# A transformer block on one core: the last 256 queries as two units of 128, with one second feed-forward product for both

## The chip, the core and the metric

The kernel runs on one core of a Trainium2 chip. The time is device microseconds (us) of one execution of the program. Beside the times of three runs there is one profiled execution, whose trace gives the start and the end of the instructions on each engine: PE (TensorE matmuls, with weight loads listed as PEld), ACT (ScalarE), DVE (VectorE), POOL (GpSimd) and SP (SyncE, which here issues every DMA).

## What is computed

A pre-norm transformer block over 2048 tokens of width 1024, in bf16:

```python
h  = x + attention(layernorm(x), wqkv, wo)     # 32 heads of 32 columns, full softmax, no mask
h2 = h + gelu(layernorm(h) @ w1 + b1) @ w2 + b2  # inner width 3584, gelu in its tanh form
```

The layer norm has no learned scale. Scores are multiplied by 32 to the power −1/2 before the softmax.

## The kernel before

**Tasks, a planner and fixed orders.** The code does not emit instructions straight away. Each call of `pe`, `mm`, `act`, `dve`, `pool` and `dma` adds a task to a graph, with the buffers that it reads and writes, an estimated duration (`c_act` for ACT, literal numbers for others), a priority and a kind (`qk`, `exp`, `pv`, `den`, `bg` for background, `warm`). `schedule` plays the graph through with these estimates and so fixes one order for each engine; `pick_pe` decides which ready task PE takes next. Two strings of digits (`PV_BEGIN`, `PV_MUST`) tell it, for each group, how many finished rounds of exponentials may pile up before P·V must run, and two tables (`GROUP_SHIFT`, `PRIO_SHIFT`) shift single tasks in the order. `merge_tiles` turns runs of narrow matmuls (four of 32 columns side by side) that are long enough into whole ones of 128. `assign` then sets the semaphores. On the chip every engine follows its fixed order and waits where a semaphore says so.

**Units, groups and rounds.** The queries are cut into `UNITS`, 8 units of 256. The heads form 8 groups of 4. For each unit and group there is a `Job` of 8 rounds. A round (`Att.qk`, L955) does 8 score matmuls, each with 32 rows of K and Q (four heads side by side in the array), into four PSUM banks, and two exponentials of 128x1024 on ACT (L966) into a buffer PT. Three pairs of score banks are used in turn. Later follow 8 narrow matmuls P·V (L1010), the sums of P over keys on DVE (L1027; for the first six units a second addition, L1033, joins two rounds) and narrow matmuls with ones for the denominators (L1050). `finish` (L1058) divides and writes OT. There are 512 rounds in all.

**What runs beside attention.** For each unit u, after its attention: `wo(u)` (product with Wo, four blocks of 512 KB, plus the residual), `ln2(u)`, `ffn1(u)` (14 blocks W1 of 256 columns; DVE adds b1 at L1206; `gelu` is made of DVE operations and a Tanh on ACT, L1229) and `ffn2(u, j, ...)` for two column halves j (14 blocks W2; DVE adds the residual at L1258, then the output DMA). These background matmuls (L660 narrow, L663 whole) fill PE between the scores of later units. They come one unit or more behind: FFN2 of unit 6 is still running when the last exponentials end.

**The lead.** Tiles x of 128 tokens are loaded by `x_tile`, normalised by `layer_norm` (DVE, with a power on POOL at L732), transposed on PE (`tr_tile`, `transposes`, L759) and copied from PSUM to xnT on ACT (L766) or DVE. `proj_half` makes Q and K of the first group in halves, `proj` and `proj_v` all other projections. `N_WARM` matmuls on constants (L1275) keep PE busy before the first tile is there.

**The tail.** The last unit, b = unit 7, is finished when no attention is left to hide it. Its W1 blocks lie in a second ring R2, whose 14 buffers are laid over the space of K and V of the groups: block i needs group i//2 to be done in b's attention. `wo(b, True)` does the first six groups (`WSPLIT`) early, and the last two, with an identity matmul that adds the residual, after the last group. `ln2(b, True)` takes its statistics from PSUM and transposes on PE (L745). `ffn1(b, ws1, True)` does its first three blocks (`HALVES`) in token halves of 128 and the others on 256; their gelu is one ACT operation straight from PSUM (L1212). `ffn2(b, ...)` puts its four results into banks 0 to 3. The whole matmuls of the tail are at L666. Unit 6 (a) goes through the ordinary path: its FFN1 loads its own 14 W1 blocks and runs during b's exponentials.

All DMAs are issued on SP in one order; a DMA that must wait for its source or its buffer holds back those behind it.

Of the kernel before, what the change touches and what calls it, by code (L numbers as in the profile page):

```python
# [7 lines left out]
ACT = mybir.ActivationFunctionType  # L8
# [59 lines left out]
class Graph:  # L68
# [267 lines left out]
    def emit(self, e, obj):  # L336
# [10 lines left out]
PV_BEGIN = "7577886548677765858856674434636846646566545566645345783555878553"  # L347
PV_MUST = "4534436267554436543436636337557333354424733246352322524333334446"
GROUP_SHIFT = (
        "0:116 1:277 2:281 4:-80 5:7 6:-257 7:-169 10:-74 14:-10 16:11 19:28 23:-117 25:-15 26:-52 27:-7 "  # L350
        "28:-94 34:-63 36:-9 44:46 46:112 47:57 52:-28 53:53 54:62 55:-11 56:1 57:-184 58:-28 60:-22 63:-28 "
        "64:16 65:-118 68:-25 70:8 76:161 79:-82 80:102 81:5 82:-25 85:27 86:-404 87:111 88:-41 90:-21 92:29 "
        "93:-269 99:-184 100:-38 103:-107 109:1 114:-32 115:20 118:-67 119:-26 120:27 121:20 122:-20 "
        "125:-349 128:2 133:-6 134:-4 135:-5 136:-96 138:-3 139:13 144:-23 145:-64 154:5 155:17 156:132 "
        "157:199 159:-154 161:12 167:-6 170:-17 171:-149 173:104 174:-24 175:117 179:-64 180:-24 188:21 "
        "189:-8 191:-351 199:-12 202:-228 205:21 206:-63 207:176 208:179 209:-139 219:28 220:-127 221:-46 "
        "223:-15 225:96 226:-29 227:-294 230:4 234:1 235:18 236:55 237:44 238:87 248:29 249:-176 253:-9 "
        "254:19 256:-139 257:-3 258:-224 260:-158 261:5 262:16 264:43 266:-2 267:14 268:9 269:157 278:-40 "
        "279:-33 280:-29 281:-23 282:-15 287:6 289:-106 290:16 291:11 293:42 294:9 297:-29 298:116 299:-16 "
        "308:-7 309:-67 310:15 311:179 312:-207 313:86 315:54 317:-242 319:-442 321:150 325:108 327:256 "  # L360
        "328:330 329:19 330:-25 331:214 332:94 336:136 337:-51 ")
PRIO_SHIFT = (
        "0:-1 2:1 4:-1 8:1 10:-1 53:1 54:1 55:-1 57:-2 58:-1 59:1 60:-3 61:-1 63:1 66:1 88:1 127:1 135:1 "
        "137:1 138:1 140:1 150:1 190:2 194:-1 196:-2 198:-1 200:-2 226:2 228:-1 258:-1 260:-2 261:-1 264:-1 "
        "267:-2 268:-2 269:-1 270:-2 271:-1 292:1 332:-1 381:1 386:-1 388:-1 389:1 390:1 392:-1 418:-1 "
        "442:-1 447:1 448:1 450:-1 472:-2 478:-1 499:-1 500:2 506:3 507:1 508:1 509:-1 527:-1 528:2 603:-3 "
        "654:1 671:1 688:1 725:-1 726:1 746:2 749:-1 770:-1 780:-1 784:1 786:-1 788:1 796:2 803:1 806:-3 "
        "810:4 815:-2 822:-1 830:-2 839:-1 840:1 841:1 842:-1 869:2 929:-1 995:-2 1062:1 1104:1 1109:1 "
        "1133:1 1144:-1 1156:-1 1161:3 1162:1 1168:-1 1174:-2 1180:-1 1198:1 1199:2 1200:1 1206:1 1208:-1 "
        "1210:-1 1213:-2 1214:1 1220:2 1222:-2 1225:3 1226:-1 1228:-1 1234:-3 1238:-1 1244:2 1249:1 1252:1 "  # L370
        "1262:-1 1265:-1 1266:-1 1268:-1 1274:1 1277:1 1278:-1 1289:-1 1290:1 1296:1 1301:2 1302:1 1303:-1 "
        "1322:2 1383:-1 1400:-1 1417:2 1422:-1 1449:-2 1458:1 1465:-1 1466:-1 1468:-3 1469:2 1472:2 1474:-1 "
        "1477:1 1483:1 1486:1 1489:-1 1494:-1 1495:1 1510:2 1517:-1 1519:1 1520:-2 1539:1 1548:-1 1557:1 "
        "1566:-1 1600:1 1636:-2 1650:-1 1654:-1 1666:-1 1671:1 1674:-1 1682:-1 1684:-1 1686:4 1688:-1 "
        "1694:-1 1702:-1 1706:1 1712:2 1723:2 1724:-1 1726:-1 1730:1 1737:1 1756:-1 1765:-1 1817:-1 1834:1 "
        "1851:-1 1859:1 1862:1 1864:1 1868:3 1876:-2 1877:-1 1880:1 1888:1 1889:1 1903:-3 1906:1 1908:-1 "
        "1917:-1 1920:2 1926:2 1932:1 1935:1 1941:-2 1951:-2 1952:-1 1953:-1 1955:-2 1973:-1 1982:-2 2000:-1 "
        "2034:-1 2051:-2 2068:-1 2076:2 2088:2 2090:-1 2093:1 2100:1 2112:1 2129:-1 2147:1 2199:-1 2233:1 "
        "2247:-1 2250:1 2281:-1 2282:1 2284:1 2285:1 2294:-1 2303:-1 2321:1 2330:2 2332:-1 2340:-3 2343:-1 "
        "2352:-1 2355:2 2356:1 2362:1 2367:-1 2368:1 2374:-2 2381:-1 2398:-1 2402:2 2404:-1 2410:-1 2420:-1 "  # L380
        "2434:1 2454:-1 2459:-1 2466:-1 2478:-1 2485:-1 2486:1 2488:-1 2499:-1 2506:-1 2520:-2 2523:1 2530:1 "
        "2534:-1 2536:1 2537:-2 2538:-2 2540:1 2582:-1 2593:-1 2594:3 2604:2 2608:-2 2628:1 2647:1 2648:2 "
        "2650:1 2651:-1 2656:-2 2659:-1 2660:1 2665:2 2670:-1 2711:-2 2743:-2 2744:-1 2754:1 2791:-1 2793:1 "
        "2794:1 2795:-1 2814:-1 2834:-2 2836:1 2837:-1 2856:-1 2874:-1 2876:2 2877:1 2878:1 2921:-1 2958:-1 "
        "2963:-1 3042:1 3043:-1 3045:-1 3046:1 3060:2 3072:1 3075:2 3084:1 3086:-1 3087:-1 3093:-1 3094:-1 "
        "3102:-2 3103:1 3116:-1 3128:2 3130:-1 3134:1 3142:-1 3146:1 3155:-1 3168:-1 3175:1 3181:1 3184:1 "
        "3187:1 3192:-1 3193:1 3209:-1 3211:1 3216:-1 3218:-1 3221:1 3222:-4 3228:-1 3233:-1 3246:-1 3248:-1 "
        "3256:1 3260:1 3261:1 3264:1 3272:1 3274:1 3281:1 3284:1 3293:1 3298:-2 3305:1 3306:-1 3315:-1 "
        "3322:1 3324:-1 3327:-2 3328:1 3330:-1 3334:-3 3340:2 3366:1 3380:-1 3390:1 3418:-1 3429:1 3430:2 "
        "3432:-1 3436:1 3496:1 3498:1 3500:-2 3533:-1 3563:1 3600:2 3604:1 3606:-2 3643:-1 3644:2 3648:-2 "  # L390
        "3688:-1 3690:-1 3730:1 3732:-2 3768:-1 3770:-2 3773:2 3792:-3 3814:-3 3816:-2 3856:1 3880:-2 "
        "3891:-2 3901:-2 3902:2 3912:1 3922:-1 3943:-1 3944:-1 3950:-2 3953:2 3958:-1 3968:1 3971:-1 3974:1 "
        "3986:1 3997:-1 4006:1 4008:-1 4012:2 4024:2 4026:-4 4038:-2 4042:-2 4050:-1 4064:-2 4065:1 4071:-1 "
        "4074:1 4083:-2 4095:-1 4098:-1 4104:-2 4105:-2 4114:-1 4117:-1 4124:1 4130:1 4132:-1 4141:-3 "
        "4142:-1 4148:1 4171:-1 4174:2 4177:1 4195:1 4201:-1 4204:-1 4211:-1 4212:-1 4213:2 4216:1 4226:-1 "
        "4235:1 4236:1 4242:-2 4244:-1 4258:1 4259:1 4262:2 4264:-1 4276:2 4306:2 4309:1 4310:-1 4312:-2 "
        "4313:-1 4314:1 4317:-1 4318:-1 4320:2 4330:-2 4332:-1 4394:1 4396:1 4398:1 4478:2 4496:2 4497:-1 "
        "4498:-2 4500:-1 4538:2 4542:-1 4580:-1 4583:1 4585:-1 4586:-1 4622:-2 4625:-1 4626:1 4665:-2 "
        "4750:-1 4763:1 4784:2 4799:-1 4807:1 4811:2 4824:-1 4828:1 4833:2 4836:-1 4845:1 4852:-3 4860:1 "
        "4861:1 4864:-2 4866:-1 4869:5 4874:-1 4875:1 4878:1 4881:1 4893:-1 4896:1 4899:2 4902:2 4908:-1 "  # L400
        "4916:1 4917:1 4922:-1 4927:1 4928:-1 4930:-1 4934:-1 4936:-1 4939:-1 4948:-7 4966:-1 4969:1 4981:-3 "
        "4984:1 4987:-1 4990:3 4999:-1 5005:-1 5012:1 5019:-1 5021:-1 5022:1 5030:-1 5034:1 5052:-1 5057:-2 "
        "5073:1 5075:2 5076:1 5078:-1 5081:2 5084:2 5086:2 5093:-1 5099:1 5102:1 5108:1 5110:2 5118:-1 "
        "5125:1 5128:-1 5148:-1 5151:-1 5158:1 5164:-1 5170:1 5174:1 5182:1 5201:-2 5202:-1 5220:-3 5222:1 "
        "5223:1 5224:-1 5225:2 5226:-1 5230:-1 5232:1 5235:-1 5236:-1 5237:-1 5239:1 5241:-1 5308:-1 5310:-1 "
        "5312:1 5314:-2 5316:2 5346:1 5375:1 5394:1 5413:1 5414:-1 5415:1 5416:-1 5459:-1 5478:-1 5499:1 "
        "5500:-1 5542:1 5604:-2 5646:1 5668:1 5674:1 5684:1 5691:1 5694:1 5700:1 5709:1 5723:-1 5726:-1 "
        "5730:1 5737:1 5740:-1 5744:-1 5746:-1 5749:-1 5750:-2 5752:-1 5761:2 5762:1 5776:1 5778:-1 5779:-3 "
        "5782:-1 5785:-1 5788:1 5797:2 5812:1 5821:-1 5824:-1 5829:1 5830:-1 5831:1 5836:1 5844:-2 5862:2 "
        "5868:-1 5882:1 5884:-1 5891:1 5897:1 5908:-1 5921:1 5935:-3 5937:-1 5942:1 5944:-1 5949:-2 5950:3 "  # L410
        "5961:-1 5962:1 5968:-2 5974:-2 5976:-1 5989:-1 5991:1 5994:-1 5997:-2 6003:1 6009:-1 6014:1 6024:1 "
# [30 lines left out]
def build_kernel(nc, A_x, A_wqkv, A_wo, B_w1, B_b1, B_w2, B_b2, out):  # L442
# [6 lines left out]
    G = D // P  # L449
    DC = D // P  # L450
    FC = F // P
    SCALE = DH ** -0.5
    EPS_BF = 1.0013580322265625e-05

    UNITS = [(256 * i, 256) for i in range(8)]
    NU = len(UNITS)

    def utiles(u):
        t0, n = UNITS[u]
        return range(t0 // P, (t0 + n) // P)  # L460

# [1095 lines left out]
```

## Time and profile before

| | |
|---|---|
| median of three runs | 1073.02 us (1071.93 to 1075.29) |
| profiled execution | 1071.41 us |
| its span in the trace | 1069.6 us |
| mean granted clock of PE in it | 0.998 |
| first scores (L955) start | 13.80 us |
| last scores start | 1006.15 us |
| last exponential ends | 1008.85 us |
| moved by DMA | 177.5 MB, mean 166 GB/s |

The span is the time from the first to the last instruction in the trace; the execution took 1.8 us more. Busy time of an engine is the union of its instructions. A group line of the profile gives line, engine, operation, the output and the inputs by the program's names, the tile, the count, then busy time, mean ns of one, and the idle time before them with what ended most of it. A line of the chain of waits gives shares of the span, followed back from the last instruction.

### The profile page before, as it was taken

Reading aid. Unit: us, or ns where it says so; the run is one execution under the profiler, and the core shown is the slowest. Engines: PE = TensorE matmul, PEld = TensorE weight load, DVE = VectorE, ACT = ScalarE, POOL = GpSimd, SP = SyncE. Lnnn points to the kernel's source line nnn. Section 1 sums busy time; section 2 is a strip of 40 time slices with the busy share of each in tenths; the row PEclk is TensorE's granted clock in tenths of the full one; section 3 lists DMA queues with packets and bytes.
Section 4 is the critical chain, followed back from the end, with each engine's and each line's share of the span. In section 5 each row is a group of like instructions: output and inputs, shape, how many; then the busy total and the mean of one; then the engine's idle time right before and its main releaser. Section 6 shows DMA issues by size and latency. Waiting matters only on the chain.

```text
span 1069.6 us, 40833 instructions
## 1 busy us (share of the span) xinstructions
PE 1028.5 (96%) x18417; PEld 593.4 (55%) x18469; DVE 836.2 (78%) x1654; ACT 1012.3 (95%) x1118; POOL 19.1 (2%) x36
## 2 busy tenths in 40 slices
PE   7899999999999999999999999999999999999998
PEld 5566645554446545744465456446645754564483
DVE  8857877777799997999699979979984986796611
ACT  5999999999999999999999999999999999999850
POOL 2100000000000000000000000000000000000000
PEclk9999999999999999999999999999999999999999
DMA  7920011004567587646776686588567745998640
GB/s 188 240 98 2 5 60 42 2 2 135 174 193 228 158 207 233 192 139 187 218 235 177 194 233 178 148 230 251 147 178 235 215 136 178 299 288 250 211 131 21
DMA packets 279999, 177.51 MB, mean 166 GB/s; under 512 B 41616, under 2 KB 274576, under 8 KB 279440
## 3 DMA queue, kind: packets, MB, share of 16 engines
q1 hardware_dynamic: 279824, 174.89, 56.5%
q8 instruction: 145, 2.38, 0.9%
q14 instruction: 30, 0.25, 0.1%
HBM read 160.96 MB, written 10.22 MB: 160 GB/s over the span
## 4 chain that ended last, share of the span: by engine, by line
ACT 70%; PE 24%; DVE 3%; DMA 2%; issue 0%; POOL 0%; POOLq 0%; SPq 0%
ACT PT L966 66%; PE ps L663 6%; PE ps L666 6%; PE ps L660 5%; PE ps L955 3%; ACT tg L1229 3%; PE ps L1010 2%; PE ps L1050 1%; DMA a_w1r<-in_B_w_dram 1%; DVE PS L1027 1%; DVE st L711 1%; DMA hnT<-a_xb 1%; PE ps L1275 1%; DMA q_scratch<-a_ost 0%; DVE xnT L768 0%
## 5 line engine op out<-in xcount | busy, mean ns | idle before, releaser
L966 ACT ACTIVATE PT<-ps 128x1024 bf16<-128x1024 f32 x996 | 924.4, 1140 | 4.1 <-PE ps L955 3.9
L1027 DVE TENSOR_TENSOR PS<-PT 128x1024 bf16<-128x1024 bf16 x425 | 288.1, 685 | 95.4 <-ACT PT L966 63.4
L955 PE MATMUL ps<-QT,KT 32*128 32x256 bf16 x4096 | 204.0, 273 | 10.1 <-ACT PT L966 4.9
L1010 PE MATMUL ps<-PT,V 128*32 128x256 bf16 x3984 | 166.9, 273 | 1.9 <-ACT PT L966 0.8
L955 PEld LDWEIGHTS ps<-QT,KT 32*128 32x128 bf16 x4096 | 61.0, 92 | 166.9 <-ACT PT L966 144.1
L663 PE MATMUL ps<-hnT,a_w1r 128*128 128x256 bf16 x1030 | 126.8, 273 | 3.9 <-DVE gT L1206 1.4
L1010 PEld LDWEIGHTS ps<-PT,V 128*32 128x32 bf16 x3984 | 101.2, 97 | 37.4 <-issue 6.5
L663 PEld LDWEIGHTS ps<-hnT,a_w1r 128*128 128x128 bf16 x1030 | 94.1, 98 | 32.2 <-issue 18.4
L660 PE MATMUL ps<-a_w2r,gT 128*32 128x512 bf16 x1560 | 110.0, 381 | 1.4 <-DVE OD L1085 1.0
L1033 DVE TENSOR_TENSOR PS<-PS 128x1024 bf16<-128x1024 bf16 x135 | 92.6, 686 | 2.5
L663 PE MATMUL ps<-a_w2r,gT 128*128 128x512 bf16 x367 | 89.7, 380 | 4.4 <-issue 2.7
L1050 PE MATMUL ps<-PS,ones 128*32 128x256 bf16 x1160 | 81.1, 274 | 0.9 <-DVE PS L1033 0.4
L660 PE MATMUL ps<-hnT,a_w1r 128*32 128x256 bf16 x2152 | 77.6, 274 | 3.2 <-DVE gT L1206 0.9
L1206 DVE TENSOR_TENSOR gT<-ps,b1f 128x512 bf16<-128x512 f32 x98 | 66.8, 686 | 13.5 <-PE ps L660 9.5
L660 PEld LDWEIGHTS ps<-hnT,a_w1r 128*32 128x32 bf16 x2152 | 52.2, 96 | 19.7 <-issue 16.0
L663 PEld LDWEIGHTS ps<-a_w2r,gT 128*128 128x128 bf16 x394 | 34.0, 98 | 45.8 <-issue 11.8
L1229 ACT ACTIVATE tg<-tg 128x1024 bf16<-128x1024 bf16 x49 | 54.7, 1144 | 0.0
L660 PEld LDWEIGHTS ps<-a_w2r,gT 128*32 128x32 bf16 x1560 | 34.8, 96 | 30.7 <-issue 16.0
L660 PE MATMUL ps<-xnT,Wall 128*32 128x512 bf16 x596 | 41.9, 381 | 0.4 <-DVE KT L820 0.3
L663 PE MATMUL ps<-Wall,xnT 128*128 128x256 bf16 x321 | 41.0, 273 | 0.0
L1050 PEld LDWEIGHTS ps<-PS,ones 128*32 128x32 bf16 x1160 | 30.9, 96 | 16.6 <-issue 5.3
L1258 DVE SCALAR_TENSOR_TENSOR b_ost<-ps,hch 128x512 bf16<-128x512 f32 x4 | 2.8, 692 | 45.0 <-PE ps L666 45.0
(99 smaller groups left out, 1022.8 us busy)
## 6 DMA issues: line engine op xcount, KB each, us to landing
a_w2r<-in_B_w_dram SPq DMA_DIRECT2D x105, 512.0 KB, 5.0
a_w1r<-in_B_w_dram SPq DMA_DIRECT2D x98, 512.0 KB, 4.6
a_w1r<-in_A_wo_dram SPq DMA_DIRECT2D x32, 512.0 KB, 4.4
b_w1r<-in_B_w_dram SPq DMA_DIRECT2D x14, 512.0 KB, 5.2
a_w1r<-in_A_wqkv_dram SPq DMA_DIRECT2D x11, 512.0 KB, 4.6
Wall<-in_A_wqkv_dram SPq DMA_DIRECT2D x16, 256.0 KB, 5.2
hch<-in_A_x_dram SPq DMA_DIRECT2D x16, 256.0 KB, 4.1
xrb<-in_A_x_dram SPq DMA_DIRECT2D x15, 256.0 KB, 4.5
```

The lines of the kernel that those rows point to most:

```text
L660: fns.append(lambda p, j=j: p.matmul(psum[32 * j:32 * j + 32, bi(bank), c0:c1], lhsT[:, 32 * j:32 * j + 32], rhs, start=start, stop=stop, ...
L663: t.whole = lambda p: p.matmul(psum[:, bi(bank), c0:c1], lhsT, rhs, start=start, stop=stop, skip_group_check=True)
L666: t = pe(lambda p: p.matmul(psum[:, bi(bank), c0:c1], lhsT, rhs, start=start, stop=stop), occ, reads=reads, writes=[bb(bank)], mode="full" ...
L711: return dve(lambda v: v.bn_stats(st_l[:, i, 6 * c:6 * c + 6], src), 0.6, reads=[B_src], writes=[B_stl[i][c]], prio=prio)
L955: return p.matmul(psum[:, 2 * us[h // 2] + h % 2, n * i:n * i + n], KT[32 * h:32 * h + 32, g, k0:k0 + P], QT[32 * h:32 * h + 32, qs, 0:n], ...
L966: act(lambda a, u=u, k=k: a.activation(pt(s)[:, k, :, :], psum[:, 2 * u:2 * u + 2, :], ACT.Exp, bias=0.0, scale=SCALE), 1024, reads=[B_ps[ ...
L1010: fns.append(lambda p, i=i, h=h: p.matmul(psum[32 * h:32 * h + 32, bi(bank), 0:nq], V[:, g, nk * r + i, 32 * h:32 * h + 32], pt(s)[:, h // ...
L1027: dve(lambda v: v.tensor_tensor(PS[:, n, :, :], pairs[:, :, 0:256], pairs[:, :, 256:512], ALU.add), c_dve(1024, 2), reads=[B_PT[2 * s], B_ ...
L1033: dve(lambda v: v.tensor_tensor(PS[:, n, :, :], PS[:, n, :, :], PS[:, m, :, :], ALU.add), c_dve(1024, 2), reads=[B_PS[n], B_PS[m]], writes ...
L1050: fns.append(lambda p, h=h, rhs=rhs, i=i: p.matmul(psum[32 * h:32 * h + 32, bi(bank), nq:2 * nq], ones32[:, :], rhs, start=False, stop=las ...
L1206: drop(dve(lambda v: v.tensor_tensor(gT[:, fc:fc + 2, cs], psum[:, bi(bank), 0:2 * n].rearrange("p (f c) -> p f c", f=2), b1f[:, fc:fc + 2 ...
L1229: act(lambda a: a.activation(t, t, ACT.Tanh, bias=0.0, scale=math.sqrt(2.0 / math.pi)), c, reads=B_t, writes=B_t, prio=-1)
```

## The change

The last unit is cut into two of 128 queries, so there are 9 units, and the last two are a (unit 7) and b (unit 8), together the old unit 7. Their jobs have 4 rounds of 16 score matmuls of 128 columns each, with 4 key blocks per round in place of 2; the number of rounds and exponentials in all stays as it was. The 14 blocks in the ring R2 (`ws1`) are now asked for before `ffn1(a, ws1)`, which uses them, and `ffn1(b, ws1, True)` uses them again. Results of `ffn1(a)` go through the DVE eviction into gT; their gelu is 7 new ACT operations of 128x512 (`late_gelu`), ordered behind the last exponential. One call `ffn2([a, b], j, ...)` serves both, with the W2 blocks that b had. The old unit 6 is an ordinary unit now, whose FFN2 takes the place of `ffn2(a)` in the code. `HALVES` goes away.

In the lead, x tile 1 is loaded in two DMAs, the transposes of the first two tiles are copied to xnT in two ACT operations of 512 each, and the first `proj_half` waits for each half on its own. `proj` and `proj_v` get a dependency on the end of the lead. `LEAD_DMA = 16` leaves a new branch in `tr_tile` unused.

The summing of P is written in a general form (`ROUNDS`, `part`, `parts`) with the same sums as before. In the planner, the estimates for an ACT operation (base 0.0615 to 0.05 us), for the power on POOL, for a warming matmul and for a change of tiling are altered, and all four tables are other ones.

```diff
-    UNITS = [(256 * i, 256) for i in range(8)]
+    UNITS = [(256 * i, 256) for i in range(7)] + [(1792, 128), (1920, 128)]
...
-        return 0.0615 + (0.093 if ap_bias else 0.0) + n / 1200.0
+        return 0.05 + (0.093 if ap_bias else 0.0) + n / 1200.0
...
+    LEAD_DMA = 16
+    B_half = [[gr.buf() for _ in range(2)] for _ in range(2)]
+    HALF = 2
...
+        if tt < HALF:
+            h = DC // 2
+            for dc in range(DC):
+                pe(lambda p, dc=dc: p.transpose(psb[:, bank, dc * P:(dc + 1) * P], xb[:, tt, dc * P:(dc + 1) * P], ident[:]),
+                   0.056, reads=[B_xb[tt], B_ident], writes=[B_ps[bank]], prio=prio)
+            for k in range(2):
+                act(lambda a, k=k: a.activation(xnT[:, tc, h * k:h * k + h, t4 * P:(t4 + 1) * P],
+                                                psb[:, bank, h * k * P:h * (k + 1) * P].rearrange("p (dc t) -> p dc t", dc=h), ACT.Copy), 512,
+                    reads=[B_ps[bank]], writes=[B_half[tt][k]] + ([B_xnTt[tc][t4]] if k else []), prio=-1)
+            return
...
-               [B_W[wp(blk)][c // P]] + B_xnTt[tc], True)
+               [B_W[wp(blk)][c // P]] + B_xnTt[tc], True, after=lead_end if dc == 0 else ())
...
-                   [B_W[wp(blk)][0]] + B_xnTt[tc][2 * h + c // P:2 * h + (c + n) // P], n > P, cols=(c, c + n))
+                   [B_W[wp(blk)][0]] + ([B_half[c // P][2 * dc // DC]] if hc == 0 and HALF else B_xnTt[tc][2 * h + c // P:2 * h + (c + n) // P]),
+                   n > P, cols=(c, c + n))
...
-                transposes_2(R.xb[s][:, :], R.B_xb[s], (4, 5), hnT[:, :, t * P:(t + 1) * P], B_hnT[t], 1 if t else -4)
+                transposes_2(R.xb[s][:, :], R.B_xb[s], (4, 5), hnT[:, :, k * P:(k + 1) * P], B_hnT[k], -4)
...
+            for f in range(2):
+                for dc in range(DC):
+                    ffn1_end[u] = mm(bank, w[:, dc, f * P:(f + 1) * P], hnT[:, dc, cs], dc == 0, dc == DC - 1,
+                       [B_w] + (B_hnT[hs[0]][2 * dc // DC:2 * dc // DC + 1] if tail else B_h), not tail, (n * f, n * f + n),
+                       after=ffn2_last if f == 0 and dc == 0 and not tail else ())
...
+    def late_gelu(u):
+        cs, hs = gcols(u)
+        for fc in range(0, FC, 4):
+            g = gT[:, fc:fc + 4, cs]
+            B_g = [B_gT[fc // 2 + k][hs[0]] for k in range(2)]
+            act(lambda a, g=g: a.activation(g, g, ACT.Gelu_apprx_tanh, bias=0.0, scale=1.0), 512, reads=B_g, writes=B_g, prio=1,
+                after=[last_exp()])
...
-    x_tile(1, -6)
+    x_tile(1, -6, 2)
...
     for j in range(2):
-        ffn2(a - 1, j, w2_blocks(R1, j))
-    ffn1(a)
+        ffn2([a - 1], j, w2_blocks(R1, j))
     ws1 = [wblock(R2, B_w1[:, 256 * i:256 * i + 256], 2) for i in range(14)]
+    ffn1(a, ws1)
     wo(b, True)
     ln2(b, True)
-    for j in range(2):
-        ffn2(a, j, w2_blocks(R1, j))
     ws2 = [w2_blocks(R2, 0), w2_blocks(R1, 1)]
+    late_gelu(a)
     ffn1(b, ws1, True)
     for j in range(2):
-        ffn2(b, j, ws2[j], banks=(2 * j, 2 * j + 1), half=False, R=R2)
+        ffn2([a, b], j, ws2[j], banks=(2 * j, 2 * j + 1), half=False, R=R2)
```

## The prediction

> **What bounds the kernel now.** I read the engine totals first, then the chain of waits, the costliest groups, the windows by stage, the waits, and last the timelines of TensorE in mid-kernel and of the end. Engine totals and chain:
>
> ```profile
> PE 1028.5 (96%) x18417; PEld 593.4 (55%) x18469; DVE 836.2 (78%) x1654; ACT 1012.3 (95%) x1118; POOL 19.1 (2%) x36
> ...
> ACT 70%; PE 24%; DVE 3%; DMA 2%; issue 0%; POOL 0%; POOLq 0%; SPq 0%
> ...
> L966 ACT ACTIVATE PT<-ps 128x1024 bf16<-128x1024 f32 x996 | 924.4, 1140 | 4.1 <-PE ps L955 3.9
> ```
>
> PE and ACT are both full. The windows (columns: stretch, length, busy time and count of PE, PEld, DVE, ACT, POOL, clock, DMA share, GB/s) say that this lasts until the exponentials end, and that afterwards PE alone works:
>
> ```profile
> 300.00:500.00 200.00, 193.81 (x3449) 108.11 (x3459) 183.21 (x356) 199.92 (x218) 2.80 (x4) 1.00 0.67 192
> 500.00:700.00 200.00, 193.92 (x3698) 109.49 (x3704) 175.13 (x335) 199.48 (x218) 1.73 (x4) 1.00 0.68 195
> ...
> 1020.00:1069.60 49.60, 46.33 (x341) 31.01 (x341) 2.77 (x4) 13.81 (x29) 0.00 (x0) 0.99 0.17 56
> ```
>
> The chain names ACT, but which of the two ends a round? A round is 8 score matmuls (L955) and two exponentials. The waits (who waits for whom; us in total, times, longest) and, below, the timeline of PE (start, length, instruction):
>
> ```profile
> PEld ps L955 <- ACT PT L966: 144.1, 421, 0.8
> ...
> ACT PT L966 <- PE ps L955: 3.9, 8, 0.7
> ```
>
> ```profile
> 444.36 0.40 PE L955 MATMUL ps<-QT,KT 32*128 32x256 bf16 x8
> 444.69 1.59 PE L663 MATMUL ps<-hnT,a_w1r 128*128 128x256 bf16 x13
> 446.21 0.40 PE L955 MATMUL ps<-QT,KT 32*128 32x256 bf16 x8
> 446.54 2.44 PE L663 MATMUL ps<-hnT,a_w1r 128*128 128x256 bf16 x20
> 448.92 0.40 PE L955 MATMUL ps<-QT,KT 32*128 32x256 bf16 x8
> ```
>
> From single starts: a matmul of 512 columns takes .2159 us, of 256 .1091, of 128 .0558 (22 of the tail's stand in 1.28 from 1017.07); four narrow matmuls (32 rows or columns each) start within .011 and take what one whole one takes; a change between row, column and full tiling costs .11. Then the round with 13 matmuls should last .22+.11+13×.1092+.11 = 1.86, and it lasts 1.85; that with 20 gives 2.62, or 2.73 with one more change, and lasts 2.71. So PE's work is the length of a round, and ACT's exponentials (pitch .904, so 1.81 per round) fit under it or fall just behind. Counted so, PE's work equals the real interval within .03 in 340 of the 479 rounds from round 32 on. Over these rounds PE's work is 889.1, ACT's .904 (and .946 for each of L1229's) sum to 912.4, the real time is 928.7: both queues are nearly full and 16.3 go where one round has too much PE work for ACT's buffers to bridge. Stretches of 16 rounds show where: in those from rounds 48, 192, 304, 352 and 480 PE's work exceeds ACT's by .85, .86, .74, 1.59, .54 (4.6 in all), and they last 1.16, 2.42, 2.38, 2.25, 2.09 (10.3) longer than ACT's.
>
> The end, last exponential to finish:
>
> ```profile
> 999.32 9.52 ACT L966 ACTIVATE PT<-ps 128x1024 bf16<-128x1024 f32 x10
> ...
> 1006.15 0.40 PE L955 MATMUL ps<-QT,KT 32*128 32x256 bf16 x8
> ...
> 1012.11 3.83 PE L663 MATMUL ps<-a_w2r,gT 128*128 128x512 bf16 x17
> ...
> 1018.80 23.51 PE L666 MATMUL ps<-hnT,b_w1r 128*128 128x128 bf16 x250
> ...
> 1042.36 12.03 PE L666 MATMUL ps<-b_w2r,gT 128*128 128x512 bf16 x54
> ...
> 1054.23 12.25 PE L666 MATMUL ps<-a_w2r,gT 128*128 128x512 bf16 x55
> ```
>
> The last scores start at 1006.15 and the span ends 63.45 later; 59.8 of that is PE work at the rates above.
>
> **The change, part by part.** Units a and b now have 128 queries each; I take the place of each step from the order of instructions the changed kernel is built with, and price it by the rows above.
>
> 1. *Does FFN1 of a run under the exponentials of b?* No. All 14 of its blocks stand on PE behind the last scores, mixed with FFN1 of b. FFN1 is bound to blocks W1 in the space of K and V of groups that b's attention still reads. So PE's end holds the same two FFN parts: FFN1 448×.0558 = 25.0 (before 96×.0558+176×.1092 = 24.6), FFN2 112×.2159 = 24.2 in both.
>
> 2. *The end otherwise.* Behind the last scores stand now: P·V sets 1.75, denominators 1.3, 39 matmuls of FFN2 of unit 6 (before 25) 8.4, identity and Wo 1.3, transposes .45, sum with FFN1 and FFN2 62.4, with tiling changes 62.9: 3.1 more than before. Added wait: the second half of b's Wo stands behind 28 matmuls of FFN2(6), 6.0, so b's layer norm and transposes come later, while FFN1(a) fills in; I find PE idle about 1 more there. Late gelu of a: 7 ACT operations over 128x512, beside 28 over 128x128. Per block of both halves ACT needs about .7 (estimate from 256 columns at .49 each), PE .89: hidden; without that cover it would add at most the 7×.6 = 4. On SP, 15 blocks of 512 KB remain to be issued after the last exponential (before 10), and an output of FFN2(6) stands among them, waiting for its eviction on DVE. At the spacing of 1.55 of the last loads before, the W1 blocks 9 and 13 land some 27 to 30 after that and are wanted at 27.5 to 29: 0 to 1.5. Sum +4.0; bounds +2.5 (idle and loads hidden) and +7 (both late).
>
> 3. *Rounds of a and b.* 16 score matmuls of 128 columns stand for 8 of 256. Sums of PE work by columns are equal (880.9 in both streams), tiling changes 1030 against 1031: 0 at .0558 a set. No row shows a set of four at 128 columns. If a set took the .109 that one of 256 takes, the 676 such sets would cost 36 more; nearest are the whole matmuls of 128 columns, each with a weight load of its own, at .0558. I take 0; below 0 is excluded, since the columns streamed are the same. [...]
>
> 4. *The new order in the exponentials.* PE's work to the last scores is 947.9, before 949.8. But it lies otherwise: rounds 32 to 111 hold 137.2 (before 143.4), rounds 112 to 127 hold 33.45 (before 28.66) against ACT's 28.93. That is scores 3.49, P·V 2.84, denominators 1.10, projections 1.75+5.61+8.73+6.48 (16 and 80 of 256 columns, 26 and 30 of 512, narrow ones counted as sets), 32 changes 3.46. One round there, 121, holds 4.2, and the next scores wait for an eviction of K. Two readings of the cost. Following each round by PE work, exponential .904, .45 from scores to exponential and 1.07 until a bank can be reused, I get 7.6 more than the same count of before gives: about 6 of it in rounds 120 to 136, the rest at 407 and 458. But that count finds only .9 of the 16.3 that the trace of before shows, so it misses the loss where PE is a little over in many rounds. By stretches, the new order has only small excesses elsewhere: from 176, 256, 352, 448, 496, of .63, .10, .35, .39, .44, 1.9 in all; at before's 10.3 per 4.6 they cost 4.3, and the large one at least its 4.5: 8.8 against 10.3, so −1.5. The ends are −2 and +8. I take +4, above the middle, since the large excess stands in one place and before's five stretches don't vanish by one.
>
> 5. *Lead in halves.* Eviction of the first transposes in two ACT copies of 512 (.6 each for one of 1.02) lets the first projection start about .4 earlier, and 5 fewer warming matmuls stand ahead. Against it, WV's first load and another DMA for the second tile stand on SP ahead of the third tile, which lands at about 8.9 (4.5 before), and its statistics stand on DVE ahead of the second tile's reciprocal. First scores at 13.0 to 14.5 (13.80 before): 0, from −1.5 to +2. FFN2 of both as one call costs nothing: two runs of 128 rows at the same 112 matmuls.
>
> Sum: 4.0+0+4+0 = +8. The profiled execution took 1071.41 with a span of 1069.6; the changed one then 1079.4. The median of the three runs, 1073.02, stands 1.6 above that execution: 1081.0. About 0.3%, or 3.2 us, is what a measurement here can tell from no change.
>
> **Rivals.** *Faster (0.12)*: the five stretches lose their 10.3 and the full rounds at 112 to 127 cost only 1, because the slack ahead of them (6.2 less PE work in rounds 32 to 111) lets PE run ahead. For it: the new order has smaller excesses everywhere else. Against: PE can lead ACT by only the score buffers, one round and a half. With the tail's +4 that is −10.3+1+4 = −5.3, or 1067.7. It decides when term 4 falls below −7.2.
> *Nothing to be seen (0.10)*: term 4 at −1.5 and lead −1.5, tail +2.5 to +4: 1072.5 to 1074, up to 1076.
> *Sets of 128 columns as dear as those of 256, or half way (0.05)*: +18 to +36 on top, though ACT's slack in the last 64 rounds hides little: 1099 to 1117. For it: the second score set starts .120 behind the first, so no faster pair is on show. Against: four starts within .011. [...]
> *Late W1 (0.06)*: the last blocks come 3 to 6 late behind the blocked output: 1084 to 1087.
> *The change does what it says*: FFN1(a) leaves the end, −12.5. The built order excludes it (under 0.01).
>
> **Numbers.** My own forecast has 0.67. All terms at their lower bounds give −1, at their upper +17; not all are there at once, so its range is 0 to +16, 1073 to 1089. From 1072 to 1090 the no-change and the late-W1 case are held too, and what is left out is the faster case and the dear sets, 0.17. Slower by over 0.3%: 0.67 + 0.05 + 0.06 = 0.78, same 0.10, faster 0.12.
>
> **What would show it.** In the profile after: no L672 matmul on b_w1r before the last scores; last scores to end 67 to 68; a stretch of ACT idle near 225 to 255 us, with waits for L983; FFN1's matmuls at .056 each; PE's wait on a b_w1r load near the end of FFN1 under 1.5. Wrong would make me: score sets of 128 columns that start .109 apart; first scores later than 15; ACT idle between 300 and 950 that falls by 7 or more, or doubles.

## The result, and the profile after

The changed kernel takes 1108.12 us (median of four runs, 1106.42 to 1109.81) against 1073.7 for the kernel before beside it: a ratio of 1.0308, 95% interval 1.0284 to 1.0332. It is slower, as forecast, but by 34 us where +8 was forecast, and above the range of 1072 to 1090.

The page of the changed kernel, the lines that answer to those shown of before, and the line of the queue that brings instructions (packets of 16 KB, MB, share of the DMA engines):

```profile
PE 1049.0 (95%) x19740; PEld 607.7 (55%) x19740; DVE 844.2 (76%) x1695; ACT 1013.4 (92%) x1124; POOL 17.8 (2%) x36
...
q8 instruction: 155, 2.54, 0.9%
...
ACT 61%; PE 32%; DVE 2%; DMA 2%; issue 2%; SPq 0%; POOL 0%; DVEq 0%
...
L994 ACT ACTIVATE PT<-ps 128x1024 bf16<-128x1024 f32 x996 | 929.6, 1165 | 29.4 <-PE ps L983 28.6
```

ACT does the same work but is idle 29.4 us ahead of exponentials (4.1 before), waiting for scores. "Issue", time in which an engine waits for nothing that the profile shows, is 2% of the chain where it was 0%. PE has 2,600 more instructions, and there are 155 fetches of code where there were 145.

Setting the first exponential of round 0, 32, 112 and so on in both traces beside each other gives the place of the 37.2 us between the two spans (1106.8 and 1069.6):

| stretch | change, us |
|---|---|
| start of round 32 (first exponential .9 earlier) | +3.6 |
| rounds 32 to 111 | −.6 |
| rounds 112 to 135 | +7.5 |
| rounds 136 to 447 | +3.0 |
| rounds 448 to 511, the units of 128 queries | +14.2 |
| from the last exponential to the end | +9.5 |

Windows over three of these stretches, before first (225 to 265, 882 to 1007, 1007 to the end), then after (228 to 274, 896 to 1034, 1034 to the end); columns as in the prediction:

```profile
225.00:265.00 40.00, 38.10 (x677) 19.22 (x672) 31.50 (x56) 40.00 (x45) 0.00 (x0) 1.00 0.23 73
...
882.00:1007.00 125.00, 120.95 (x2229) 66.86 (x2231) 90.45 (x176) 123.63 (x135) 1.10 (x2) 1.00 0.84 244
1007.00:1069.60 62.60, 59.00 (x472) 38.48 (x469) 11.78 (x33) 19.85 (x38) 1.35 (x2) 0.99 0.32 104
```

```profile
228.00:274.00 46.00, 44.60 (x748) 24.72 (x744) 32.69 (x59) 40.04 (x44) 0.00 (x0) 1.00 0.15 49
...
896.00:1034.00 138.00, 124.97 (x3445) 77.96 (x3433) 93.23 (x213) 124.34 (x134) 1.65 (x3) 0.99 0.78 215
1034.00:1106.80 72.80, 65.54 (x888) 44.04 (x886) 16.63 (x41) 18.90 (x42) 0.55 (x1) 1.00 0.47 143
```

Around 228 to 274 ACT has lost 6 us and PE is full: PE binds. In 896 to 1034 both engines are idle for 13 us (PE 4, ACT 1.4 before): something stops PE that is not ACT, and ACT then waits for scores. The timeline of PE in this stretch shows where (idle time and its cause in brackets):

```profile
1019.21 0.28 PE L1076 MATMUL ps<-PS,ones 128*32 128x128 bf16 x8
1019.32 0.33 PE L1037 MATMUL ps<-PT,V 128*32 128x128 bf16 x10
1022.35 0.29 PE L1037 MATMUL ps<-PT,V 128*32 128x128 bf16 x6 [2.69 <-issue]
1022.42 1.17 PE L669 MATMUL ps<-a_w2r,gT 128*32 128x512 bf16 x12
1023.52 0.61 PE L983 MATMUL ps<-QT,KT 32*128 32x128 bf16 x16
```

PE stops for 2.7 us in the middle of one task: 10 of its 16 P·V matmuls are done, and the other 6 have the same inputs and need no wait. ACT is idle 3.1 ahead of its next exponential. Counting PE's records (matmuls and weight loads), the eight gaps of this kind of over .55 us after 900 us stand at:

```
gap at   length  records so far   since the last
 908.52   1.28      31519
 938.36   0.77      33052         1533 = 6 x 255.5
 947.30   1.62      33561          509 = 2 x 254.5
 975.08   1.67      35088         1527 = 6 x 254.5
 990.25   0.58      35851          763 = 3 x 254.3
 993.65   1.74      36107          256
1019.65   2.70      37383         1276 = 5 x 255.2
1038.34   2.50      38148          765 = 3 x 255.0
```

Four smaller ones (.25 to .51) fit the same steps; all twelve sum to 14.5 us. The steps answer to the fetches of code: the whole trace has 155 of them for 39,480 such records, one for 254.7. A fetch of code is one packet of 16,384 bytes, .88 to 2.48 us long (median .96); in each of these gaps PE goes on 2.2 to 3.2 us after the start of a fetch. By and large, the later that fetch starts, the longer PE stands: with 109 recorded instructions still ahead of PE the gap is 1.28, with 44 it is 1.67, with none 2.50 and 2.69 (but with 155 at 947.30 it is 1.62). The kernel before has two such gaps of over .25 from 60 us on, .9 us in all. That is theory 1 below: PE runs out of code.

### The profile page after: what moved, and what is told of

Same layout as the page of the kernel before. It is cut to its first block, busy times and chain, and to the rows that moved or that the text cites. A ratio compares the mean times of both kernels' runs of the same rounds, so it can differ in the third digit from the quotient of the medians.

```text
span 1106.8 us, 43508 instructions
## 1 busy us (share of the span) xinstructions
PE 1049.0 (95%) x19740; PEld 607.7 (55%) x19740; DVE 844.2 (76%) x1695; ACT 1013.4 (92%) x1124; POOL 17.8 (2%) x36
## 4 chain that ended last, share of the span: by engine, by line
ACT 61%; PE 32%; DVE 2%; DMA 2%; issue 2%; SPq 0%; POOL 0%; DVEq 0%
ACT PT L994 56%; PE ps L672 11%; PE ps L669 7%; PE ps L983 5%; PE ps L1037 4%; PE ps L675 4%; ACT tg L1259 3%; PE ps L1076 2%; ACT PX L994 1%; DMA a_w1r<-in_B_w_dram 1%; DMA b_w1r<-in_B_w_dram 1%; DMA xrb<-in_A_x_dram 1%; SPq L696 0%; DVE PS L1054 0%; PE ps L768 0%
## 5 line engine op out<-in xcount | busy, mean ns | idle before, releaser
L994 ACT ACTIVATE PT<-ps 128x1024 bf16<-128x1024 f32 x996 | 929.6, 1165 | 29.4 <-PE ps L983 28.6
L983 PE MATMUL ps<-QT,KT 32*128 32x256 bf16 (+1 forms) x4608 | 205.6, 261 | 18.9 <-ACT PT L994 7.8
L1037 PE MATMUL ps<-PT,V 128*32 128x256 bf16 (+1 forms) x4496 | 165.9, 261 | 12.3 <-issue 9.3
L1037 PEld LDWEIGHTS ps<-PT,V 128*32 128x32 bf16 x4496 | 105.3, 97 | 44.1 <-issue 15.7
L672 PE MATMUL ps<-a_w2r,gT 128*128 128x512 bf16 x516 | 125.4, 381 | 0.7 <-DVE OD L1108 0.4
L1236 DVE TENSOR_TENSOR gT<-ps,b1f 128x512 bf16<-128x512 f32 (+1 forms) x112 | 73.2, 653 | 26.7 <-PE ps L672 18.4
L1076 PE MATMUL ps<-PS,ones 128*32 128x256 bf16 (+1 forms) x1312 | 77.9, 260 | 4.3 <-issue 1.7
L669 PE MATMUL ps<-a_w2r,gT 128*32 128x512 bf16 x1072 | 79.7, 385 | 0.5 <-DVE a_ost L1287 0.3
L672 PEld LDWEIGHTS ps<-a_w2r,gT 128*128 128x128 bf16 x516 | 44.7, 98 | 59.3 <-issue 11.6
L672 PE MATMUL ps<-xnT,Wall 128*128 128x512 bf16 (+1 forms) x196 | 46.6, 368 | 0.4 <-DVE OD L1111 0.2
L672 PE MATMUL ps<-a_w1r,OT 128*128 128x512 bf16 x181 | 45.0, 381 | 0.2
L1076 PE MATMUL ps<-PT,ones 128*32 128x256 bf16 (+1 forms) x792 | 32.3, 256 | 2.0 <-issue 1.3
```

The lines of the kernel that those rows point to most:

```text
L669: fns.append(lambda p, j=j: p.matmul(psum[32 * j:32 * j + 32, bi(bank), c0:c1], lhsT[:, 32 * j:32 * j + 32], rhs, start=start, stop=stop, ...
L672: t.whole = lambda p: p.matmul(psum[:, bi(bank), c0:c1], lhsT, rhs, start=start, stop=stop, skip_group_check=True)
L983: return p.matmul(psum[:, 2 * us[h // 2] + h % 2, n * i:n * i + n], KT[32 * h:32 * h + 32, g, k0:k0 + P], QT[32 * h:32 * h + 32, qs, 0:n], ...
L994: act(lambda a, u=u, k=k: a.activation(pt(s)[:, k, :, :], psum[:, 2 * u:2 * u + 2, :], ACT.Exp, bias=0.0, scale=SCALE), 1024, reads=[B_ps[ ...
L1037: fns.append(lambda p, i=i, h=h: p.matmul(psum[32 * h:32 * h + 32, bi(bank), 0:nq], V[:, g, nk * r + i, 32 * h:32 * h + 32], pt(s)[:, h // ...
L1076: fns.append(lambda p, h=h, rhs=rhs, i=i: p.matmul(psum[32 * h:32 * h + 32, bi(bank), nq:2 * nq], ones32[:, :], rhs, start=False, stop=las ...
```

## The experiments

**Is it code?** Four kernels on one chip: the changed one again; the kernel before with each narrow matmul of attention made two in the last unit, or in the last four; and the changed kernel with every two of them made one in a and b.

> The changed kernel itself, on the same chip as the three beside it. Every theory: 1106 to 1110 us, 1.03 of the time before; PE gaps of 1.3 to 2.7 us, a multiple of some 255 PE instructions apart, after 900 us (13 us in all in the trace that is already there).

Measured: 1112.34, ratio 1.0332 (1.0289 to 1.0374), with gaps in the same places (1.61 at 908.0, 1.40 at 1019.6, 1.57 at 1035.8). The median is above the 1106 to 1110 expected; the kernel before is slower here too, 1075.89.

```diff
-            for i in range(nk):
+            w = P if qb >= SPLIT else n
+            for i, c in [(i, c) for i in range(nk) for c in range(0, n, w)]:
                 for h in range(4):
...
+    SPLIT = 7
...
```

These lines are for the scores, with P = 128; P·V and the denominators are halved in the same way. For split4, `SPLIT` is 4.

> The kernel before, its order of tasks untouched; only in the last unit each narrow matmul of 256 columns (scores, P.V, denominators) is two of 128, so PE has the same columns in twice the instructions there. Theory 1, PE runs out of code: the fetches of PE code cannot keep up where sets of 128 columns stand together; +8 to +14 us (1081 to 1087), PE gaps of 1 to 3 us behind 900 us that stand a multiple of some 255 instructions apart, sets of 128 still start .056 us apart. Theory 2, a set of four at 128 columns takes the .109 us of one at 256: +18 to +36 us, starts .11 apart, no gaps. Theory 3, the loss is all from the new order: 0.

Measured: 1094.23, ratio 1.0175 (1.0142 to 1.0209), +18.8 us; 21 of its profile's growth lie in rounds 448 to 511. Its timeline of PE:

```profile
973.87 0.62 PE L660 MATMUL ps<-hnT,a_w1r 128*32 128x256 bf16 x16
974.32 0.28 PE L1013 MATMUL ps<-PT,V 128*32 128x128 bf16 x6
977.25 0.34 PE L1013 MATMUL ps<-PT,V 128*32 128x128 bf16 x10 [2.65 <-issue]
```

Nothing of before's order was touched, so theory 3 falls for this part. The size is above what theory 1 gave and at the low end of theory 2, so the lengths of sets must decide: four P·V matmuls of 128 columns start .056 behind the four before them (median), sets of scores .055 to .068. Theory 2 falls. The nine largest gaps sum to 15 us.

> As split7, but in the last four units, 256 rounds instead of 64. Theory 1: four times the rounds, but with more whole matmuls of the feed-forward parts between them, so 2 to 4 times the loss of split7: +16 to +56 us, and the number of code fetches rises by the added instructions over 255. Theory 2: +70 to +144. Theory 3: 0.

Measured: 1145.83, ratio 1.0671 (1.0624 to 1.0717), +72 us: more than I gave theory 1, and near theory 2's lower end, again with P·V sets at .056 and score sets at .055 to .067. 184 fetches against 145: 39 more, and 10,123 added instructions over 255 are 39.7. Forty-four gaps of over .25 on "issue", each 143 to 162 records past 255 times the number of the last fetch, sum to 54; what the rest of the 72 is was not separated. That ACT's time to refill after a gap is one part was not shown.

```diff
-            for i in range(nk):
+            for i in range(2):
                 for h in range(4):
-                    k0 = (nk * r + i) * P
+                    k0 = (nk * r + nk // 2 * i) * P
...
-                        return p.matmul(psum[:, 2 * us[h // 2] + h % 2, n * i:n * i + n],
...
+                        return p.matmul(psum[:, 2 * us[h // 2] + h % 2, 256 * i:256 * i + 256],
...
```

These lines are for the scores; P·V and the denominators go the same way. In a and b, where nk is 4, this kernel leaves out every second key block and streams 256 columns against each of the others. It no longer computes the attention of a and b, and serves for the time alone.

> The changed kernel, its order of tasks untouched; in the two units of 128 queries every two narrow matmuls of 128 columns are one of 256 (the second key block of each pair is left out and its columns are taken from the neighbouring ones), so PE streams the same columns in half the instructions there. Theory 1: the gaps go, -11 to -14 us against the changed kernel (1094 to 1097). Theory 2: -18 to -36. Theory 3: 0.

Measured: 1093.62, ratio 1.0165 (1.0125 to 1.0204). Against the changed kernel beside it that is 1.0165/1.0332, 1.6% or 18 us less, about what split7 adds. That is more than the 11 to 14 of theory 1 and just in the range of theory 2, which the lengths of the sets rule out. Its profile gets 13.8 back in rounds 448 to 511 and 2.8 behind them. The DMA view over those rounds, first of the changed kernel, then of this one:

```profile
q8 instruction: 27, 0.44, 1.3%
```

```profile
q8 instruction: 18, 0.29, 0.9%
```

and its timeline of PE, where three such rounds pass without a gap on "issue":

```profile
1007.03 0.40 PE L983 MATMUL ps<-QT,KT 32*128 32x256 bf16 x8
1007.36 0.61 PE L669 MATMUL ps<-a_w2r,gT 128*32 128x512 bf16 x8
1007.80 0.61 PE L1037 MATMUL ps<-PT,V 128*32 128x256 bf16 x16
1008.23 0.28 PE L1077 MATMUL ps<-PS,ones 128*32 128x256 bf16 x4
```

So about half of the loss is code. The other half lies in the order, the lead and the end.

**What crowds rounds 112 to 127?** The tables are written for one graph, so I took the kernel before with both shift tables empty as a base and added single edits.

> The kernel before with both shift tables empty, the base for the three beside it. Its order has 30.5 us of PE work in rounds 112 to 127 (28.7 with the tables) and 64.2 behind the last scores (59.8). By the count of rounds +1 in the rounds and +4.4 at the end: 1076 to 1083 us.

Measured: 1079.56, ratio 1.0043 (1.0026 to 1.006), as expected.

```diff
...
-               [B_W[wp(blk)][c // P]] + B_xnTt[tc], True)
+               [B_W[wp(blk)][c // P]] + B_xnTt[tc], True, after=lead_end if dc == 0 else ())
...
```

and the same in `proj_v`.

> plain, and projections of Q, K and V depend on the end of the lead as in the changed kernel; nothing else. Rounds 112 to 127 then hold 35.2 us of PE work against ACT's 28.9. Theory A, work that is put off in the first rounds meets its due time at round 128 and PE then holds ACT up: +4 to +6 against plain, in ACT gaps near rounds 112 to 130. Theory B, the score buffers and the slack before it bridge it: 0 to +1.

Measured: 1091.08, ratio 1.0142 (1.0114 to 1.0171), 1.0% above plain. The timeline of ACT, plain first:

```profile
224.01 31.40 ACT L881 ACTIVATE PT<-ps 128x1024 bf16<-128x1024 f32 x34
257.17 18.66 ACT L881 ACTIVATE PT<-ps 128x1024 bf16<-128x1024 f32 x20 [1.76 <-PE ps L870]
```

```profile
224.31 31.48 ACT L882 ACTIVATE PT<-ps 128x1024 bf16<-128x1024 f32 x34
263.20 11.11 ACT L882 ACTIVATE PT<-ps 128x1024 bf16<-128x1024 f32 x12 [7.41 <-PE ps L871]
```

Theory A: the exponentials stop for 7.4 at round 128 where they stopped for 1.8. Of 9.8 in the profile 5.8 are in rounds 112 to 127; the time is twice what I expected, the rest is spread behind.

```diff
-        return 0.0615 + (0.093 if ap_bias else 0.0) + n / 1200.0
+        return 0.05 + (0.093 if ap_bias else 0.0) + n / 1200.0
```

> plain, and only the planner's base estimate of an ACT operation is 0.05 us in place of 0.0615, as in the changed kernel. The order then has 37.4 us of PE work in rounds 112 to 127 and 79.2 behind the last scores (plain 64.2), and 17 less in rounds 128 to 447. Theory A: +7 to +10 near rounds 112 to 130, ACT as the bound in rounds 128 to 447 so that the 17 less give back at most 8 of small losses, and +15 at the end: +14 to +25 against plain. Theory B: the 17 that PE saves there pay for the end: 0 to +8.

Measured: 1101.03, ratio 1.0244 (1.0219 to 1.0268), 2.0% or 21 us above plain: by the profile 10.7 in rounds 112 to 127, then 5.9 given back up to round 448, 5.3 lost in the last 64, and 14.4 at the end. Theory A. Either edit alone makes the crowd in a kernel without tables; which of them the changed kernel's own tables leave standing was not tried.

**What do the units cost by themselves?** `UNITS`, `ws1` for both, `late_gelu` and the one `ffn2` of the changed kernel on plain:

> plain with the units of 128 queries, the shared W1 blocks, the late gelu and the one FFN2 of the changed kernel, but with the lead, the planner's estimates and the first 448 rounds of plain, which hold the same PE work to a tenth of a us. Theory 1, code fetches: +15 to +20 in the last 64 rounds and the first part of the end, and 0 to +4 for the end itself: +15 to +24 against plain, gaps of 1 to 3 us on PE a multiple of some 255 instructions apart. Theory 3, the loss of the changed kernel came from its order elsewhere: 0 to +4.

Measured: 1108.33, ratio 1.0296 (1.0257 to 1.0335), 2.5% or 27 us above plain, over the 15 to 24 of theory 1. Its profile: 15.7 in the last 64 rounds as theory 1 expected, but 15.5 behind them. There, beside one gap of 3.5 on code, nine blocks of FFN1(a) in a row wait .52 to .61 each for the DVE eviction of the block ahead, 5.2 us.

> plain_units with every two narrow matmuls of 128 columns of the last two units made one of 256 (the second key block of each pair is left out, its columns are taken from the neighbouring ones): what is left of the units and their end without the code fetches. Theory 1: the 16 of the last 64 rounds and 3 to 4 of the end go, so 17 to 20 less than plain_units, and 8 to 12 above plain, all of it behind the last scores. Theory 3: no change against plain_units.

Measured: 1092.13, ratio 1.0139 (1.0119 to 1.0158): 1.5%, 16 us, below plain_units, 1.0%, 10 us, above plain. It leaves out every second key block of a and b as merged does. Its profile is 16.2 above plain's: 10.8 behind the last exponential, nothing in the last 64 rounds, and 5.6 in the 448 rounds before, which hold the same PE work in both. Without its code stalls the change still loses at the end.

**The lead.** In the changed kernel the 512 KB of WV are issued ahead of x tiles 2 to 7. One entry of `PRIO_SHIFT` does it:

```diff
-18:-1 53:1
+53:1
```

> The changed kernel, and only one entry of its priority table is dropped (18:-1), so that the first 512 KB of WV are issued behind the x tiles 2 to 7 again, as in the kernel before. Lead theory (the third x tile comes late behind WV and starves the exponentials of rounds 4 and on): x tile 2 lands 4 us earlier, the ACT gap of 2.5 us at 27.5 goes, and round 32 starts 2 to 4 us earlier than the changed kernel's 81.6. Rival (the lead is slow for the order of its DVE and ACT steps): round 32 within 1 us of 81.6. Behind it everything as in the changed kernel.

One execution, 1103.51 beside 1073.39: round 32 starts at 79.6 against 81.6. The ACT gap at round 4 goes from 2.5 to 1.6, not away. So WV's place costs some 2.0 of the 3.6. This rests on one profile each: traces whose orders agree that far start round 32 at 81.1 to 81.6 (the changed kernel twice, merged), and at 77.8 to 79.2 (before, split4, split7), so about 1 us of such a difference can be variation.

> plain_units with the halves of the lead (x tile 1 in two DMAs, the first transposes copied in two ACT operations, the first projection by halves) and nothing else; no shift tables, so WV stays behind the x tiles. If the halves do what they say: first exponential .5 to 1.0 us earlier (plain_units as plain: 15.0), and still .3 to 1 us at round 32. Rival (bound further on by the layer norms of the next tiles on DVE): earlier at round 0, nothing left at round 32.

One execution, 1107.76: first exponential at 13.5 against 15.1, round 32 at 76.3 against 79.3, 3.0 earlier. The halves do what they say, and more, where WV stays behind, as far as one profile of each shows it.

> The kernel before, with its own tables, estimates and units, and only the halves of the lead from the changed kernel; WV stays behind the x tiles, and both halves of x tile 1 stand ahead of tile 2. From round 32 on the order holds the same PE work as before. If the gain that the halves showed beside plain_units (3.0 us at round 32) carries over: round 32 at 75 to 77 against 78.0, and 0.997 to 0.999 of the time before. Rival (the chained rounds behind take it back, since PE binds many of them): the first scores earlier, the time within 0.1%.

Measured over five rounds: 1075.38, ratio .9997 (.9984 to 1.0009). The first exponential is .7 earlier, round 32 only .1 (77.9). The rival's outcome, but not its mechanism: beside before's tables the gain is gone within the lead, where round 4 starts at 25.9 instead of 25.2. A likely reason, not tried, is that x tile 2 stood ahead of tile 1 there and is now behind it. No version here beats the kernel before.

## Why the prediction was right and wrong

The direction was right, and it does not hang on the cost that was missed: merged, with little left of the stalls, is still 1.0165 of before. The first step was right too: no FFN1(a) matmul runs before the last scores; the first starts at 1050.76, 16.6 behind them. The size fell on these terms.

*Term 3, rounds of a and b, taken at 0: measured some 18* (by the profiles 13.8 in the rounds and 2.8 at the end). This is the step that failed most. I priced columns streamed and tiling changes, and kept the bound of 36 for a set as long as one of 256 columns. The sets are not longer: .056, and .055 to .068 for scores, as the row of whole matmuls (.0558) promised. What doubled is the number of instructions, a cost that I had not listed at all.

How this stops PE is shown in part. Two fetches never start closer than 3.35 us in before's trace and 3.36 in the changed kernel's, 13 ns for each of some 255 matmuls and weight loads. But that spacing is not what binds in the gaps: the fetches that end the changed kernel's twelve start 4.2 to 8.3 us after the fetch before. They come late, with 178 recorded instructions or fewer ahead of PE, which goes on 2.2 to 3.2 us after they start. A set of four P·V matmuls with its four weight loads takes .109 at 256 columns, 13.6 ns an instruction; at 128 columns .056, 7 ns. By these rows 100 to 200 instructions would last 1.4 to 2.7 us in wide sets and .7 to 1.4 in narrow ones (an estimate), so narrow sets would run out of code more often; that is argued, not shown. What sets the start of a fetch is open.

The rival "sets of 128 as dear, or half way" gave 1099 to 1117, where the time fell, but for a reason that the traces refute.

*Term 4, the order, taken at +4 from −2 to +8: measured +10* (rounds 32 to 447), of which 7.5 stand out from variation. Following each round had given 7.6 more than before, with about 6 of it in rounds 120 to 136, and the trace has 7.5 in 112 to 135, in those places:

```profile
241.97 1.94 ACT L994 ACTIVATE PT<-ps 128x1024 bf16<-128x1024 f32 x2 [0.50 <-PE ps L983]
245.06 3.77 ACT L994 ACTIVATE PT<-ps 128x1024 bf16<-128x1024 f32 x4 [1.15 <-PE ps L983]
250.92 7.44 ACT L994 ACTIVATE PT<-ps 128x1024 bf16<-128x1024 f32 x8 [2.09 <-PE ps L983]
```

The second reading, that before's five stretches with 10.3 would shrink and pay for it, was wrong: rounds 136 to 447 became no shorter, +3.0. I had averaged a count that names its rounds with a proportion that names none. The +3.0 itself is no finding: split7 and before_lead, which hold before's PE work there, take 2.6 and 3.6 more than before over the same rounds, each in its one profile. For the same reason a sign named ahead says little here: ACT's idle time between 300 and 950 did more than double, from 1.8 to 8.3, but 4.3 of that lie behind 896, among the gaps on code, and split7 has 3.5 between 300 and 886 where before has .9.

*Term 2, the end, taken at +4.0 from 2.5 to 7: measured 9.2* from the last scores (72.6 against 63.45). 14 more matmuls of FFN2(6) are 3.0, as worked out; code is 2.8; FFN1 takes 28.8 where before it took 25.3. The timeline of PE:

```profile
1050.76 1.07 PE L672 MATMUL ps<-hnT,b_w1r 128*128 128x128 bf16 x16 [0.42 <-DVE a_ost L1287]
1052.39 1.07 PE L672 MATMUL ps<-hnT,b_w1r 128*128 128x128 bf16 x16 [0.56 <-DVE gT L1236]
```

FFN1(a) takes its banks from the pool, and its next block waits until DVE has emptied one. I had asked which engine is busier per block, and not which bank the next block gets. In the changed kernel that costs PE a long wait only once, .7 from start to start, since blocks of b fill in from 1053 on. The rest of the 3.5 is the wait for late W1 blocks, pauses of .07 to .16 between blocks, and the transposes, which stand in this stretch. In plain_units, where nothing fills in, the wait stands at nine blocks in a row. The matmuls themselves run at .0559 (104 in 5.81); the wait for late W1 loads is .8 on PE, within the 0 to 1.5 given.

*Term 5, the lead, taken at 0 from −1.5 to +2: measured +3.6* at round 32. Two things that I had seen with opposite signs do act: the halves bring the first exponential .9 earlier, and WV ahead of the third x tile costs some 2.0. What the remaining 2.5 are was not separated; about 1 us of it can be variation.

The rival on the other side, five stretches that give back 10.3, did not come; nothing of its mechanism is seen.

## What to carry to other kernels

Count instructions as well as columns: halving every narrow matmul of the last unit doubled their number, and at the same columns split7 had 10 more fetches (155 against 145) and took 18.8 us longer. The sign here was a gap on "issue" in the middle of one task (2.69 us in the changed kernel, 2.65 in split7); see whether such gaps lie a fixed number of instructions apart (some 255 here), and test it by splitting operations in the unchanged kernel and by joining them in the changed one. Before a small difference between two traces is explained, look what kernels with the same order differ by in that stretch. In a kernel with a planned order, a count of work per stretch against the other engine names the places of a loss well; trust it over a proportion drawn from other stretches.

## What was not expected of the hardware

One fetch brings 16,384 bytes, and two fetches never started less than 3.35 us apart in before's trace, or 3.36 in the changed kernel's. In the changed kernel's gaps PE went on 2.2 to 3.2 us after a fetch had started, though its packet takes about 1 us (median .96). Of the 35 fetches of its last stretch (from 890 on), 19 start when PE still has 100 to 200 recorded instructions of code ahead, counted to 155 records past 255 times the fetch's number, where the gaps stand (151 to 157); two (at 1019.8 and 1038.6) start only when it already stands. Why these start late is open.
